# A retention layer and a snake-activated feed-forward layer on one core: a new order of the program up to block 1

## The chip, the core and the metric

The kernel runs on one core of one Trainium2 chip. The core has a matrix engine (PE, with its weight loads shown as PEld), a vector engine (DVE), a scalar engine (ACT), a general engine (POOL) and a sequencer that mostly issues DMAs (SP). Each engine works through its own list of instructions in order and waits on semaphores where it needs another's result. ACT, POOL and SP also issue DMAs from their lists. PE writes into PSUM, which the kernel uses as eight banks; POOL does not read them here. The metric is the time of one execution in microseconds (us), as the device counts it.

## What is computed

Shapes: q, k, v are 8 batches x 8 heads x 576 positions x 64. The output has 4608 rows (8 x 576) of 512. Cut to what matters:

```python
scores = scale * np.matmul(q, k.transpose(0, 1, 3, 2))
Dmat = np.where(rel >= 0, gamma[:, None, None] ** rel[None, :, :], 0.0)
attn_out = np.matmul(scores * Dmat, v)
x = attn_out.transpose(0, 2, 1, 3).reshape(B * S, H * D)    # 4608 x 512
h = x @ w_in                                                # 512 x 2048
g = h + np.sin(alpha * h) ** 2 / (alpha + 1e-09)
out = g @ w_out                                             # 2048 x 512
```

gamma is one number per head. Inputs and output are float32.

## The kernel before

Attention is done in chunks of 128 positions with a running state. For a batch b, the first 512 positions are handled as two halves p = 0, 1 of 256 positions, each two chunks; the last 64 positions of all batches form a ninth block at the end. The decay gamma^(i-j) is split into a factor on k and a factor on q, which a *cast* from float32 to float16 multiplies in.

For each batch and half the steps are: *load* k, q, v from HBM (512 KB each, on SP's list, into six rotating raw buffers, so that a load waits until the buffer six loads back has been cast); *cast* them (on V, that is DVE, on A_, that is ACT, or on G_, that is POOL; `ys=(0,)` or `(1,)` takes one half of the heads); *turn* k and q (PE transposes into a bank, 8 matmuls or 4 for one half) and *take* them back into SBUF (`kT`, `qT`); *outer* (64 x 64 products of k and v, the new sum of each chunk); *take_sum* or *evict* (the sum into `kvs`); *more* or *next_sum* (add the decayed former sum: two POOL instructions, or four DVE instructions); *to_state* (the sum times a factor, float16); *scores* (PE, for heads' half y, 16 matmuls); *masked* (DVE, the triangular mask, 128 x 1024 elements); *values* (PE, two passes) and *add_states* (PE, the state times q); *keep* (the result into `xT`, the input of the next layer). From batch 2 on the transposes of k and q are DMA transposes (*crossed*).

The feed-forward layer works on blocks n of 512 rows. *project(n, u)* makes unit u of 16 (128 of the 2048 hidden columns): four matmuls of 512 columns, into one PSUM bank; a third argument gives the bank (`op`, `h0`, `h1`, `h2`, `m0`, `m1`), a fourth one half of the rows. Then *sine* (ACT), *square* (ACT, DVE or POOL), *product* (DVE) write `gT`. *gemm2(n, u)* is the second layer for blocks 0 and 1: u = 4 c + part adds the hidden units 4 part to 4 part + 3 to output rows c, four matmuls of 512 columns; *finish* copies and stores a bank. Blocks 2 to 8 use a scheme with seven half-sized products in place of eight (`Quarters`), whose sums of weights *weigh* forms, on POOL mostly.

The weights are loaded by POOL: *load_w_in(g)* brings the columns of units 4 g to 4 g + 3, *load_w_out(g)* the rows of hidden units 4 g to 4 g + 3 (so gemm2 with part g), each 1 MB of float32 read and 512 KB of float16 written.

Nothing schedules the program: `tc.manual_schedule()` keeps the instructions of each engine in the order in which the Python calls stand, from line 740 on. The list up to line 1242 is written out by hand, block by block with batches ahead of it; a loop makes blocks 3 to 7. *keep_busy* issues matmuls on zeros, to fill PE. *told(last, eng)* puts an empty instruction on `eng` that waits for the instruction `last`; what follows on that engine waits with it.

Lines that matter here: load 121, cast 181 (k, q) and 104/102 (v, on DVE or POOL / on ACT), turn 215, outer 298, copies 102 and 104, next_sum 327, to_state 332, more 339 and 340, scores 358, masked 370, values 400, add_states 422, project 535, sine 543, square 552 (ACT) and 554, product 559, gemm2 581, weigh 602, load_w_in 92, load_w_out 95, keep_busy 696.

In the list before, batch 0's second q half is cast by POOL in one piece, w_in(0) and w_in(2) are issued after it, then `more(1)`; the first state of batch 0 is made on DVE; batch 1's second half of q is cast and turned while batch 0 is still being masked; the units of blocks 0 and 1 come in mixed orders (block 0: 2, 1, 0, 8, 3, 11, 6, 7, 5, 4, 12, 14, 9, 10, 15, 13).

## Time and profile before

| | us |
|---|---|
| median of 3 runs | 299.51 |
| lowest and highest | 299.17, 302.67 |
| the profiled execution | 301.28 |
| its span, first to last instruction | 299.6 |
| PE busy | 284.6 (95%) |
| DVE busy | 223.6 (75%) |
| ACT busy | 207.3 (69%) |
| POOL busy | 200.5 (67%) |

The mean granted clock of PE over the span is 0.983 of full speed.

How to read what follows. A *row of the timeline* gives start, duration, engine, source line, operation, the tiles (written <- read), shapes, how many instructions were merged, and in brackets how long the engine had been idle and what ended that. "SPq" is an instruction of SP's list. The *chain of waits* is followed back from the last instruction: each piece is the work that the next one waited for. A *list of waits* names who waited for whom: us in total, how often, the longest. A *table of stages* gives, for each stretch, the busy time of each engine, the granted clock, and the share and rate of the DMA engines. A *group* ("x14 | 10.1, 742 | 1.7") gives the count, the busy time in all, the mean ns of one and the idle time before. "DMA to landing" is the time from issue until the last byte was there.

### The profile page before, as it was taken

To read this page: it belongs to the slowest core of one execution; us is meant where nothing else is said; L and a number is where in the kernel's file an instruction comes from. 1 tells how busy PE (TensorE), PEld (TensorE's weight loads), DVE (VectorE), ACT (ScalarE), POOL (GpSimd) and SP (SyncE) were. 2 spreads that over 40 slices of the span, in tenths; PEclk is the share of its full clock that TensorE was granted. 3 is DMA by queue.
4 is the path that set the end of the run, shared out by engine and by line. 5 is a ranking of instruction groups with operands and counts; after the bars stand their busy time and mean duration, and the time that the engine had idled before them with its cause. 6 is when DMAs were issued, how large, how long until landed. Compare 5 with 4: busy or idle time off the path is not lost.

```text
span 299.6 us, 8720 instructions
## 1 busy us (share of the span) xinstructions
PE 284.6 (95%) x3597; PEld 185.3 (62%) x3597; DVE 223.6 (75%) x313; ACT 207.3 (69%) x330; POOL 200.5 (67%) x188
## 2 busy tenths in 40 slices
PE   7649999999999999989999999999999999999993
PEld 6536555554544576666666666766666666665782
DVE  1596899879867897998679867876778476656871
ACT  1434983886756799776878787878777878887600
POOL 5691675899999998898788889769923900370000
PEclk9787999999999999999999999999999999999999
DMA  7999999599888298878697977687866201310225
GB/s 220 341 216 216 279 233 287 151 287 287 229 172 263 63 153 185 225 194 191 152 267 184 190 189 204 57 183 161 151 137 145 53 3 39 71 37 16 62 49 120
DMA packets 119159, 49.89 MB, mean 167 GB/s; under 512 B 69824, under 2 KB 118096, under 8 KB 119120
## 3 DMA queue, kind: packets, MB, share of 16 engines
q1 hardware_dynamic: 114528, 45.04, 63.8%
q0 software_dynamic: 4224, 4.19, 8.3%
q8 instruction: 28, 0.46, 0.6%
q10 hardware_dynamic: 368, 0.11, 0.2%
q14 instruction: 11, 0.09, 0.1%
HBM read 36.74 MB, written 9.44 MB: 154 GB/s over the span
## 4 chain that ended last, share of the span: by engine, by line
PE 81%; DVE 6%; ACT 3%; POOL 3%; issue 2%; DMA 2%; SPq 1%; DVEq 0%; ACTq 0%
PE hps L535 37%; PE hps L652 27%; PE ops L581 9%; PE o L400 3%; ACT s_t L543 2%; PE sc L358 2%; DMA q<-in_q_dram 2%; DVE ret L370 2%; DVE gT L559 2%; DVE s L332 1%; PE kv L298 1%; SPq L121 1%; PE o L422 1%; POOL k L181 1%; POOL q L181 1%
## 5 line engine op out<-in xcount | busy, mean ns | idle before, releaser
L559 DVE SCALAR_TENSOR_TENSOR gT<-ss_t,inva,hps 128x512 f16<-128x512 f16 x144 | 105.5, 743 | 37.4 <-ACT ss_t L552 35.9
L543 ACT ACTIVATE s_t<-hps,alpha_t 128x512 f16<-128x512 f32 x144 | 96.5, 682 | 38.5 <-PE hps L535 37.8
L535 PE MATMUL hps<-xT,w_in 128*128 128x512 f16 (+1 forms) x564 | 121.4, 361 | 1.0 <-DVE gT L559 0.7
L535 PEld LDWEIGHTS <-w_in 128*128 128x128 f16 x628 | 60.5, 98 | 53.3 <-issue 1.8
L552 ACT ACTIVATE ss_t<-s_t 128x512 f16<-128x512 f16 x118 | 73.8, 630 | 3.2
L652 PEld LDWEIGHTS <-gT 128*128 128x128 f16 x656 | 63.9, 98 | 14.4
L624 POOL TENSOR_TENSOR gT<-gT,d 128x1024 f16<-128x1024 f16 x12 | 25.2, 2121 | 31.2 <-PE hps L652 30.2
L652 PE MATMUL hps<-T,gT 128*128 128x256 f16 x336 | 39.8, 273 | 0.0
L652 PE MATMUL hps<-w_out,gT 128*128 128x256 f16 x320 | 38.2, 273 | 0.0
L370 DVE TENSOR_TENSOR ret<-sc,mask 128x1024 f16<-128x1024 f32 (+1 forms) x32 | 34.8, 1115 | 3.0 <-PE sc L358 3.0
L672 DVE TENSOR_TENSOR osb<-osb,hps 128x512 f32<-128x512 f32 x35 | 24.0, 685 | 14.8 <-PE hps L652 14.1
L581 PE MATMUL ops<-w_out,gT 128*128 128x512 f16 x128 | 30.5, 379 | 0.2 <-ACT kvs L102 0.2
L181 POOL TENSOR_TENSOR q<-q,cn 128x1024 f16<-128x1024 f32 (+1 forms) x16 | 27.0, 1696 | 4.3 <-DMA q<-in_q_dram 4.3
L630 POOL TENSOR_TENSOR gT<-gT 128x1024 f16<-128x1024 f16 x12 | 26.1, 2195 | 0.0
L181 POOL TENSOR_TENSOR k<-k,cn 128x1024 f16<-128x1024 f32 (+1 forms) x13 | 21.9, 1684 | 2.3 <-DMA k<-in_k_dram 2.3
L581 PEld LDWEIGHTS <-gT 128*128 128x128 f16 x128 | 12.0, 98 | 13.9 <-issue 0.2
L340 POOL TENSOR_TENSOR kvs<-s,kvs 128x256 f32<-128x256 f32 x22 | 17.1, 777 | 2.5 <-ACT kvs L102 0.8
L102 ACT CAST xT<-o 128x1024 f16<-128x1024 f32 (+1 forms) x14 | 13.2, 956 | 6.5 <-PE o L422 6.5
L102 ACT COPY osb<-hps 128x512 f32<-128x512 f32 (+2 forms) x15 | 8.2, 548 | 13.6 <-PE hps L652 13.4
L332 POOL TENSOR_TENSOR s<-kvs,cn 128x256 f16<-128x256 f32 x21 | 13.4, 643 | 4.7 <-ACT kvs L102 4.0
L554 DVE TENSOR_TENSOR ss_t<-s_t 128x512 f16<-128x512 f16 x22 | 13.9, 631 | 3.3 <-ACT s_t L543 3.2
L535 PE MATMUL hps<-xS,w_in 128*128 128x512 f16 x64 | 15.0, 379 | 0.0
(78 smaller groups left out, 274.3 us busy)
## 6 DMA issues: line engine op xcount, KB each, us to landing
out_dram<-osb SPq DMA_DIRECT2D x70, 128.0 KB, 2.5
q<-in_q_dram SPq DMA_DIRECT2D x16, 512.0 KB, 5.7
k<-in_k_dram SPq DMA_DIRECT2D x10, 512.0 KB, 7.3
v<-in_v_dram SPq DMA_DIRECT2D x10, 512.0 KB, 6.0
k<-in_k_dram SPq DMA_DIRECT2D x24, 128.0 KB, 3.5
v<-in_v_dram SPq DMA_DIRECT2D x24, 128.0 KB, 3.5
w_in<-in_moe_w_in_dram POOLq DMA_DIRECT2D x4, 512.0 KB, 11.0
w_out<-in_moe_w_out_dram POOLq DMA_DIRECT2D x4, 512.0 KB, 10.2
```

The source lines that it names most:

```text
L102: eng.copy(d_, s_)
L181: eng.tensor_tensor(dst[:, a0:a1].rearrange("p a r t d -> p t (a r) d"), t_.rearrange("p (t a) x -> p t a x", t=2)[:, :, a0:a1].rearrange( ...
L370: nc.vector.tensor_tensor(ret.rearrange("p t (z x) -> p (t z) x", z=2)[:, :, 0:n], sc.rearrange("p t (z x) -> p (t z) x", z=2)[:, :, 0:n], ...
L535: matmul(hps_of[n, fc][0][:, cols], w_in16[:, a, fc * P : (fc + 1) * P], xs[n][:, a, cols], start=(a == 0 and part != 1), stop=(a == KT - ...
L543: nc.scalar.activation(s_t, hps, mybir.ActivationFunctionType.Sin, bias=0.0, scale=alpha_t[:, fc : fc + 1],)
L552: nc.scalar.activation(ss_t, s_t, mybir.ActivationFunctionType.Square)
L559: nc.vector.scalar_tensor_tensor(gT[n][:, :, fc, :], ss_t.rearrange("p (t n) -> p t n", t=2), inva[:, fc : fc + 1], hps.rearrange("p (t n) ...
L581: matmul(ops[n, c, cols.start][:, cols], gT[n][:, c // 2, fk, c % 2 * P : c % 2 * P + P], w_out16[:, fk, cols], start=(fk == 0), stop=(fk ...
L624: eng.tensor_tensor(self.part(0, 0, i), self.part(1, 1, i), self.d3[:, 4 * i : 4 * i + 4], SUB)
L630: eng.tensor_tensor(out_, self.part(1, 0, i), self.part(0, 0, i), SUB)
L652: matmul(self.ps[name][:, 256 * m + cols.start : 256 * m + cols.stop], left(j)[:, P * m : P * m + P], right(j)[:, cols], start=(tag is not ...
L672: nc.vector.tensor_tensor(out_, a, self.ps[ps], ADD)
```

## The change

The list from the first load to the end of block 1 is written anew; the rest changes only in unit numbers and in two gemm2 units that now stand earlier. `cast` returns its instruction, so that an engine can be made to wait for it, and batch 1's halves get the q buffers in natural order. In words:

- Batch 0 is cast, turned and taken by halves of the heads: k and q of the first half on DVE, v on DVE and ACT; the second q on POOL in two pieces, the second k on DVE in two. All six loads of batch 0 are issued first and the six of batch 1 directly behind them.
- An empty instruction makes POOL wait for the cast of the first q; then POOL issues w_in(0) and w_in(1), ahead of the second q. w_in(2) and (3) follow among batch 0's states, w_out(0) in block 0's unit 2, w_out(1) in unit 5, w_out(2) and (3) behind a cast of batch 1's first v.
- The states and all sums of batch 0 and batch 1 are made by POOL (`to_state`, `more`); the copies of batch 0's second sums stand ahead of keeping its first values.
- Batch 1 is turned and attended after block 0's projections, among fourteen gemm2 units of block 0 (nine before).
- Blocks 0 and 1 take their units in the order 0 to 15; in block 1, three gemm2 units of block 1 and two of block 0 stand where eight stood.

```diff
-    order_of_q = [(0, 0), (0, 1), (1, 1), (1, 0), (2, 0), (2, 1), (3, 1), (3, 0), (4, 1), (4, 0)]
+    order_of_q = [(0, 0), (0, 1), (1, 0), (1, 1), (2, 0), (2, 1), (3, 1), (3, 0), (4, 1), (4, 0)]
...
-            eng.tensor_tensor(
+            return eng.tensor_tensor(
...
         load(0, "k", 0)
         load(0, "q", 0)
-        cast(0, "q", 0, V, (1,))
+        load(0, "v", 0)
+        load(0, "q", 1)
+        load(0, "k", 1)
+        load(0, "v", 1)
+        cast(0, "k", 0, V, (0,))
         cast(0, "k", 0, V, (1,))
-        cast(0, "k", 0, G_, (0,))
...
         keep_busy(16, "h0", 256)
-        keep_busy(44, "op", 64)
+        keep_busy(14, "op", 64)
+        turn(0, "k", 0, "op", (0,))
+        take(0, "k", 0, A_, (0,))
+        keep_busy(3, "h0", 128)
+        turn(0, "k", 0, "op", (1,))
+        take(0, "k", 0, A_, (1,))
+        cast(0, "q", 0, V, (0,))
+        told(cast(0, "q", 0, V, (1,)), G_)
+        load_w_in(0)
+        load_w_in(1)
+        turn(0, "q", 0, "h2", (0,))
+        take(0, "q", 0, A_, (0,))
+        keep_busy(4, "h0", 128)
+        turn(0, "q", 0, "h2", (1,))
+        cast(0, "v", 0, V, (0,))
+        cast(0, "v", 0, A_, (1,))
+        take(0, "q", 0, V, (1,))
         at[0].outer((0,), "h0", "h1")
...
+        at[0].scores(0, 0, "m0")
+        at[0].scores(0, 1, "m1")
+        turn_alpha()
+        at[0].take_sum(0, A_)
+        take_alpha()
+        at[0].take_sum(1, A_)
+        at[0].masked(0, 0)
+        cast(0, "q", 1, G_, (0,))
+        cast(0, "q", 1, G_, (1,))
+        keep_busy(5, "h2", 256)
+        turn(0, "q", 1, "op", (0,))
+        take(0, "q", 1, A_, (0,))
+        at[0].to_state(0, G_)
+        cast(0, "k", 1, V, (0,))
+        cast(0, "k", 1, V, (1,))
+        turn(0, "k", 1, "h2", (0,))
+        take(0, "k", 1, A_, (0,))
+        turn(0, "q", 1, "op", (1,))
+        take(0, "q", 1, A_, (1,))
+        at[0].masked(0, 1)
+        turn(0, "k", 1, "h2", (1,))
+        take(0, "k", 1, V, (1,))
+        keep_busy(4, "h0", 256)
+        load(1, "k", 0)
+        load(1, "q", 0)
+        load(1, "v", 0)
+        load(1, "k", 1)
+        load(1, "q", 1)
+        load(1, "v", 1)
+        at[0].more(1)
+        cast(0, "v", 1, A_, (1,))
+        cast(0, "v", 1, G_, (0,))
+        at[0].scores(1, 1, "m0")
+        at[0].to_state(1, G_)
         load_w_in(2)
...
+        at[0].outer((1,), "h2", "op")
+        at[0].scores(1, 0, "m1")
+        at[0].masked(1, 1)
         at[0].masked(1, 0)
...
+        at[0].values(0, False, "h0", "h1")
         at[0].values(0, True)
         at[0].add_states(0)
+        at[0].take_sum(2, A_)
+        at[0].take_sum(3, A_)
+        at[0].keep(0, A_, A_)
+        at[0].more(2)
+        at[0].to_state(2, G_)
+        load_w_in(3)
+        at[0].values(1, False, "m0")
         at[0].values(1, True)
         at[0].add_states(1)
+        at[0].keep(1, A_, V)
+        project(0, 0, "op", 0)
+        project(0, 1, "h2", 0)
         invert_alpha()
+        at[0].more(3)
+        project(0, 0, "op", 1)
...
+        project(0, 4, "m1")
+        product(0, 2)
+        sine(0, 4)
+        cast(1, "k", 0, G_, (0,))
+        square(0, 4, G_)
+        project(0, 5, "m0")
+        sine(0, 5)
+        square(0, 5, A_)
         load_w_out(1)
...
+        project(0, 12, "h2")
+        sine(0, 12)
+        cast(1, "q", 0, G_, (0,))
+        square(0, 12, G_)
...
+        gemm2(0, 4, "op")
+        gemm2(0, 12, "h2")
+        turn(1, "q", 0, "m1")
         product(0, 15)
...
+        gemm2(0, 0, "h0")
+        at[0].to_state(3, G_)
+        at[1].scores(0, 0, "m0")
+        gemm2(0, 5, "op")
+        at[1].scores(0, 1, "m1")
+        at[1].masked(0, 0)
         at[1].masked(0, 1)
...
+        gemm2(0, 13, "h2")
+        cast(1, "v", 0, G_, (0,))
+        cast(1, "v", 0, A_, (1,))
+        load_w_out(2)
+        load_w_out(3)
+        gemm2(0, 1, "h0")
...
+        at[1].outer((0,), "m0")
+        at[1].evict((0,), A_)
+        cast(1, "k", 1, G_)
+        at[1].to_state(0, G_)
+        at[1].values(0, False, "m1")
+        at[1].values(0, True)
+        turn(1, "k", 1, "h1")
+        take(1, "k", 1, A_)
+        cast(1, "q", 1, V)
...
+        turn(1, "q", 1, "m0")
+        take(1, "q", 1, V)
         at[1].more(1)
         at[1].to_state(1, G_)
+        weigh(1, 0, G_)
+        cast(1, "v", 1, A_)
+        gemm2(0, 8, "h1")
+        at[1].scores(1, 1, "m0")
+        at[1].scores(1, 0, "m1")
+        at[1].masked(1, 1)
+        at[1].masked(1, 0)
+        gemm2(0, 9, "h1")
         gemm2(0, 6, "op")
+        at[1].outer((1,), "m0")
+        at[1].evict((1,), A_)
+        at[1].more(2)
+        at[1].to_state(2, G_)
+        gemm2(0, 14, "h2")
         at[1].values(1, False, "m1")
         at[1].values(1, True)
+        gemm2(0, 2, "h0")
         at[1].add_states(1)
         at[1].keep(1, A_)
+        gemm2(0, 10, "h1")
+        gemm2(0, 15, "h2")
+        finish(0, 3, V)
+        weigh(1, 1, G_)
+        gemm2(0, 7, "op")
...
+        project(1, 0, "m0", 0)
+        project(1, 0, "m0", 1)
...
+        project(1, 1, "h2")
+        square(1, 0, V)
+        sine(1, 1)
+        gemm2(0, 3, "h0")
...
+        gemm2(0, 11, "h1")
+        finish(0, 2)
...
-        gemm2(0, 8, "h1")
-        sine(1, 1)
+        gemm2(1, 0, "h1")
+        sine(1, 9)
...
-        gemm2(0, 9, "h1")
-        sine(1, 2)
+        gemm2(1, 1, "h1")
+        sine(1, 12)
...
-        gemm2(0, 10, "h1")
-        gemm2(0, 11, "h1")
-        finish(0, 2)
+        gemm2(1, 2, "h1")
...
         at[3].outer((0, 1), "m1")
         product(2, 3)
-        gemm2(1, 1, "h1")
-        gemm2(1, 2, "h1")
         at[3].evict((0, 1), A_)
```

More of the change, by code (lines that the diff above doesn't have):

```diff
@@ L781 @@
-        keep_busy(10, "h2", 256)
-        take(0, "q", 1, A_)
-        load(1, "q", 1)
-        at[0].take_sum(1, V)
-        at[0].more(1)
-        cast(0, "v", 1, V)
-        at[0].to_state(1, V)
-        load_w_in(1)
-        at[0].to_state(0, V)
-        at[0].outer((1,), "h2", "h1")
-        cast(1, "q", 1, G_)
-        at[0].masked(0, 1)
-        at[0].scores(1, 0, "m0")
-        turn(1, "q", 1, "op")
-        at[0].masked(0, 0)
-        at[0].masked(1, 0)
-        at[0].scores(1, 1, "m1")
@@ L901 @@
-        at[1].outer((0,), "h0", "h2")
-        at[1].masked(0, 1)
-        sine(0, 13)
-        at[1].scores(0, 0, "m1")
-        gemm2(0, 12, "h0")
-        gemm2(0, 13, "h0")
-        at[1].take_sum(0, A_)
-        at[1].take_sum(1, A_)
-        square(0, 13, A_)
-        at[1].masked(0, 0)
-        product(0, 13)
-        load(1, "v", 1)
-        turn(1, "k", 1, "h2")
-        take(1, "k", 1, V, (1,))
-        take(1, "k", 1, V, (0,))
-        gemm2(0, 14, "h0")
-        at[1].scores(1, 1, "m0")
@@ L918 @@
[L918 to L924 removed]
+        take(1, "q", 0, A_, (0,))
+        take(1, "q", 0, V, (1,))
+        gemm2(0, 0, "h0")
[4 more added lines that the diff above has]
+        at[1].masked(0, 0)
+        at[1].masked(0, 1)
```

309 lines of the change are left out of this document (111 added, 198 removed).

## The prediction

> **What bounds the kernel now.** I read first how long TensorE (PE) waited, then the stages, then the chain of the first 30 us, then the single rows. Waits of PE, in the first 28.3 us and from there to 113 us:
>
> ```profile
> PE sc L358 <- DVE ret L370: 3.8, 1, 3.8
> ...
> PE ops L581 <- ACT kvs L102: 0.2, 1, 0.2
> PE o L400 <- issue: 0.2, 1, 0.2
> ```
>
> Busy time by stage (columns: stretch, length, PE, weight loads, DVE, ACT, POOL, granted clock, DMA share, GB/s):
>
> ```profile
> 9.80:13.20 3.40, 3.21 (x59) 2.77 (x48) 2.04 (x4) 1.50 (x2) 3.13 (x3) 0.50 1.14 344
> 13.20:16.40 3.20, 3.10 (x83) 2.39 (x82) 1.90 (x4) 2.00 (x3) 3.08 (x5) 1.00 1.19 286
> 16.40:20.00 3.60, 0.00 (x0) 0.00 (x0) 3.60 (x3) 0.37 (x1) 3.52 (x4) 1.00 1.19 215
> 20.00:25.40 5.40, 5.03 (x128) 3.95 (x128) 4.76 (x5) 1.01 (x1) 3.53 (x4) 0.50 1.20 217
> 28.30:53.70 25.40, 25.06 (x345) 14.16 (x344) 23.33 (x44) 18.61 (x32) 15.00 (x17) 1.00 1.16 261
> 53.70:77.00 23.30, 23.30 (x245) 12.19 (x243) 20.52 (x27) 17.71 (x31) 22.83 (x22) 1.00 0.93 240
> 77.00:105.00 28.00, 27.73 (x471) 14.34 (x471) 21.39 (x27) 18.59 (x31) 27.61 (x29) 1.00 0.70 179
> ```
>
> From 28.3 to 113 us PE waits 0.4 us by the list: nothing that keeps its matmuls can gain there. All that can be gained lies ahead of 28.3 us, where PE stands still for 3.6 us (16.4 to 20.0) and then runs at half the clock. The chain of waits there:
>
> ```profile
> 4.00 6.01 DMA q<-in_q_dram
> 10.07 1.90 POOL q L181
> 11.97 1.47 POOL w_in L92 x2
> ...
> 15.41 3.50 DVE s L332 x2
> 18.92 3.41 DVE ret L370 x3
> ```
>
> Not a load but POOL's queue and DVE set the pace: the cast of q's second half, two weight DMAs issued ahead of a state sum, two states, four masks. The states' 3.50 us is odd:
>
> ```profile
> 15.41 3.50 DVE L332 TENSOR_TENSOR s<-kvs,cn 128x256 f16<-128x256 f32 x2 [1.30 <-POOL kvs L340]
> 16.15 1.91 POOL L181 TENSOR_TENSOR q<-q,cn 128x1024 f16<-128x1024 f32 x1
> 18.01 0.61 POOL L339 TENSOR_TENSOR s<-kvs,cn 128x256 f32<-128x256 f32 x1
> 18.84 4.72 DVE L370 TENSOR_TENSOR ret<-sc,mask 128x1024 f16<-128x1024 f32 x4
> L332 DVE TENSOR_TENSOR s<-kvs,cn 128x256 f16<-128x256 f32 x1 | 0.4, 417 | 0.0
> ```
>
> The same instruction takes 417 ns in a later stage; here the pair ends only after both POOL instructions, and the masks follow.
>
> **The change part by part.** I take it as one chain from batch 0's loads to T0, the start of block 0's first projection; from there I let PE run as densely as before from 28.3, and then look for what breaks that.
>
> *Batch 0.* The first six loads keep their order. The rows for the start:
>
> ```profile
> 5.57 1.04 POOL L181 TENSOR_TENSOR k<-k,cn 128x512 f16<-128x512 f32 x1 [1.47 <-DMA k<-in_k_dram]
> 7.03 0.69 DVE L181 TENSOR_TENSOR q<-q,cn 128x512 f16<-128x512 f32 x1 [5.80 <-DMA q<-in_q_dram]
> 8.51 1.04 ACT L102 CAST v<-v 128x1024 f16<-128x1024 f32 x1 [4.79 <-DMA v<-in_v_dram]
> 11.91 1.68 POOL L92 DMA_DIRECT2D w_in<-in_moe_w_in_dram  x2
> L121 SPq DMA_DIRECT2D k<-in_k_dram x1: 1460/1460/1460, 5.5 to 5.5; - x1
> DMA to landing us min/median/max: 6.0/6.0/6.0
> ```
>
> k, q and v are there at 5.6, 7.0 and 8.5, the second k at 5.5 + 6.0 = 11.5. DVE casts k's halves by 6.9 and q's by 8.3 (0.69 each). With turns, copies and v's halves on DVE and ACT about 9.5, the outer products run at 9.6 and both scores end by 11.1; before, the same scores were masked from 18.84. The first mask (4.72/4 = 1.2) runs 10.7 to 11.9. Then DVE casts the second k's halves while POOL casts the second q's halves (1.04 each, 10.1 to 12.1) and goes on to the states. If DVE gets its turn between two POOL instructions, the casts end at 13.8; mask 15.0, copy 15.4, scores 15.9, two masks 18.3, values 19.4. POOL's last state needed (to_state(2)) is about as late, 19.5. So T0 is 19.7.
>
> The row of 3.50 us says DVE may be passed over more than once, to about 14.8, and T0 to 20.7. The Trainium skill, "SBUF — State Buffer", section "SBUF: two separate sides", calls the port pair of the two engines an exclusive lock held for a whole instruction, which by itself gives the 19.7; the row, where DVE also sat out the second POOL instruction, measures worse than that. I take 19.7, since POOL here has gaps (it waits for sums); both ends stay in the range.
>
> *The weights.* The marker makes POOL wait for the second q cast (8.3); behind it stand w_in(0), w_in(1), q's casts, all states. Issued at 8.3 in place of 11.9, w_in(0) comes 3.6 us sooner:
>
> ```profile
> L92 POOL DMA_DIRECT2D w_in<-in_moe_w_in_dram x4: 746/804/942, 11.9 to 19.4; - x4
> DMA to landing us min/median/max: 7.8/11.0/11.8
> L121 SPq DMA_DIRECT2D v<-in_v_dram x1: 1350/1350/1350, 11.5 to 11.5; - x1
> DMA to landing us min/median/max: 14.1/14.1/14.1
> ```
>
> The first of the four needed the least, 7.8; the last, issued at 19.4, came 11 to 12 later: 19.7 to about 30.8, 3.7 apart. So w_in(0) now lands at 16.1, ahead of T0, and the next five weights, issued in time behind it, at about 20, 23.5, 27, 31 and 35, where units 4, 8 and 12 and the first gemm2 of either half want them at T0 + 3.5, 7, 10.5, 14.5 and 18: ahead each time. The price is paid by SP's queue, on which batch 1's six loads now stand directly behind batch 0's: rates fall from 344 to 215 GB/s when weights flow, and the v load issued at 11.5 needs 14.1 us where the k load at 5.5 needed 6.0. Batch 0's last v (due at 13.0) can lose up to some 2 us; its cast is needed by 15, so I cost it at 0, with 1.5 as the other end. Batch 1's first k, q and v are wanted at about T0 + 4, T0 + 10.6 and T0 + 15.5, and I put them at 22, 29.5 and 35: just in time. w_out(2) and (3), issued only after batch 1's first v is cast (about 36), would land near 45 and 49 at some 9 us and 4 us more (estimates from w_in's landing and the throttled rate), and the multiplications that need them come at 46 and 52: cover of 1 us, no more.
>
> *Block 0 and batch 1.* Sixteen projections in order, then fourteen gemm2 units among batch 1's attention, in place of nine. A unit of four matmuls costs 0.86:
>
> ```profile
> 59.12 0.86 PE hps L535 x4
> L559 DVE SCALAR_TENSOR_TENSOR gT<-ss_t,inva,hps 128x512 f16<-128x512 f16 x14 | 10.1, 742 | 1.7 <-ACT ss_t L552 1.5
> L554 POOL TENSOR_TENSOR ss_t<-s_t 128x512 f16<-128x512 f16 x4 | 4.1, 1036 | 10.6 <-ACT s_t L543 10.6
> ```
>
> DVE needs 16 x 0.742 plus five squares and a few copies, about 15.4 against PE's 13.8 plus turns; the lag of 1 to 2 us is taken up by six banks and by the gemm2 units that follow, so 0. No matmul of use is added or dropped. keep_busy costs nothing where PE would wait anyway; the units moved ahead of block 1 leave it (three gemm2 fewer, 20.7 of PE) with DVE at 20.5: DVE cannot hide less than that. Cost 0 to 2.6; I take 0.4.
>
> *POOL.* Net of what leaves it (half a cast of k, batch 1's q: 2.9), it gains two squares, two half casts of v, three sums and four states, about 9.3; so +6.4. Its waits before were longest at the squares (10.6 in the row above), so there is room in block 0. Before, this was its entry into batch 2:
>
> ```profile
> 53.39 4.09 POOL L104 CAST v<-v 128x1024 f16<-128x1024 f32 x2 [3.51 <-DMA v<-in_v_dram]
> 57.45 4.49 POOL L602 TENSOR_TENSOR T<-w_out 128x512 f16<-128x512 f16 x4
> 61.90 1.90 POOL L181 TENSOR_TENSOR q<-q,cn 128x1024 f16<-128x1024 f32 x1
> ```
>
> After, half of the T's (weigh(1, 0), 2.2) stands in a gap ahead, and from the copy of batch 1's last sums (25 units of 0.86, some 6 us of batch 1's small matmuls and the copy after T0: 48.1) come two sums and two states (3.9), the other half of the T's and the casts of v, 3.1 to 4.1: the q cast starts at 57.3 to 58.3 in place of 61.90. From there POOL is full: 22.83 of 23.30 and 27.61 of 28.00.
>
> *The sum.* Before, from 28.3 to the end of the span (299.6) is 271.3, with one unit of block 0 (0.86) and one of batch 1's four turns already done, which at full clock costs what the next one did:
>
> ```profile
> 31.77 0.61 PE L215 MATMUL tr<-ident,q 128*128 128x128 f16 x8
> ```
>
> After: 19.7 + 271.3 + 0.9 + 0.6 = 292.5, a gain of 7.1. Off that, 0.4 for DVE in block 1 and 0.3 for the clock (below): 6.4. The profiled execution took 301.28 with 299.6 as its span, 1.8 above the median of the runs, 299.51. Against the median, 299.51 - 6.4 = 293.1.
>
> **The rivals.** *POOL holds part of it back.* PE gains 7.1 by the sum, but POOL only 3.6 to 4.6 (61.9 less 58.3 or 57.3); if nothing in its full stretch to 105 us has slack, that less the clock's 0.3 stays: 295.2 to 296.2, and 297.2 with T0 at 20.7. Against it: in 28.3 to 113 us no wait of PE names POOL, and
>
> ```profile
> 73.43 1.18 POOL L332 TENSOR_TENSOR s<-kvs,cn 128x256 f16<-128x256 f32 x2
> 78.18 0.51 PE L422 MATMUL o<-qT,s 64*64 64x128 f16 x24
> ```
>
> batch 2's last state is ready 3.6 us ahead of the matmuls that read it (78.18 less 74.61).
>
> *POOL becomes the bound: slower.* The same engine, but its added 6.4 us finds no idle time, because in block 0 it waits in order behind casts of late loads. Then the cast of batch 2's second q starts at 61.9 + 6.4, and with 3.6 of slack the end moves by +2.8: 302.3. It decides once that cast starts after 65.5. Where DVE keeps interrupting POOL as it was itself held, the tail reaches past 305.5. For it: 98% busy; against it: ten us of idle time from 28.3 to 53.7 alone (15.00 of 25.40 busy).
>
> *The clock.* Batch 0 is now chopped into quarter steps with idle time between. The rows: the 3.6 us of standing still from 16.40 were followed by half clock (0.50 for 5.4 us), and the 3.40 us from 9.80, most of it turns, by full clock.
>
> ```profile
> 9.80:13.20 3.40, 2.90 (x24) 0.42 (x1) 1.50 (x2) 0.50 1.14 344
> ```
>
> (That is the turns' own tile: 2.90 of 3.40.) By these rows turns hold the clock up and the gaps after the change, at most 1.4, are short: 0.3. If they do not, PE starts block 0 at half clock for some 6.8 us, losing 3.4: 296.5. The Trainium skill, "TensorE: Matmul & The Clock Gate", "Part 4: PE-mode transpose", says that transposes do not count as busy for the clock; by that rule this case would come about, but the trace disagrees (1.00 after 9.80:13.20).
>
> **How the numbers follow.** My forecast has 0.58: 293.1, its own range 291 to 295.5 (from T0 half a us sooner and nothing taken off, 291.9, with the runs' own scatter below that, to T0 at 20.7 and half of DVE's 2.6). The faster bound, 2%, lies at 293.5; 0.45 of the 0.58 lies under it, since the late ends have to meet to pass it, 0.13 above. POOL holding back 0.16, the clock 0.10: both within 2%. POOL as the bound has 0.16, of which 0.12 beyond 305.5, where a POOL that cannot recover over 50 us ends, and 0.04 within. Faster by over 2% (about what a measurement of this kernel can tell from no change) 0.45, within 0.13 + 0.16 + 0.10 + 0.04 = 0.43, slower 0.12. The range for eight in ten runs from 291 to 298: it holds the first three cases and leaves out the slower one.
>
> **What would show it.** Right: the first projection on PE near 19.7 to 20.7; w_in(0) landed at 16; the four masks spread over 10.7 to 18.3; clock 1.00 from then on; PE's waits from T0 to block 2 under 1.5 us; POOL's first full q cast of batch 2 near 57. Wrong: a wait of PE on a DMA'd weight near gemm2 units 6 or 15, a POOL wait on k or q of batch 1, half clock in block 0, a projection's wait on DVE in block 1, or POOL late at that cast. A first projection after 23 would refute the chain for batch 0 as a whole.

## The result and the profile after

The change made the kernel slower. Three runs of the changed kernel took 313.15 to 315.29 us, 314.19 in the median, against 299.51 before: a ratio of 1.046, with an interval of 1.034 to 1.058. The prediction had 293.1 with a range up to 298. The span of the profiled execution after is 312.4; before it was 299.6.

The longest of PE's waits from 18 us to the end (total, times, longest, in us), of the changed kernel:

```profile
PE hps L535 <- DVE gT L559: 5.3, 3, 3.2
PE o L422 <- POOL s L332: 3.6, 2, 3.5
PE hps L535 <- issue: 1.6, 1, 1.6
PE sc L358 <- DMA qT<-q: 0.8, 1, 0.8
PE hps L652 <- DVE osb L672: 0.7, 1, 0.7
```

Before, the stretch from 28.3 to 113 us held 0.4 us of waits. Now there are long single ones: 3.2, 3.5 and, later, 1.6 us. The table of stages, after:

```profile
13.20:16.40 3.20, 2.30 (x101) 1.77 (x104) 2.68 (x4) 1.88 (x5) 3.12 (x5) 1.00 1.18 212
16.40:20.00 3.60, 2.51 (x82) 1.97 (x75) 1.63 (x3) 1.66 (x3) 3.40 (x6) 1.00 1.17 258
28.30:53.70 25.40, 21.81 (x292) 10.44 (x294) 17.51 (x21) 12.07 (x18) 16.87 (x21) 0.93 1.10 247
53.70:77.00 23.30, 22.16 (x232) 11.11 (x223) 18.72 (x25) 17.00 (x28) 12.35 (x12) 1.00 0.79 172
77.00:105.00 28.00, 23.97 (x326) 11.46 (x327) 17.05 (x22) 13.80 (x22) 27.29 (x30) 0.88 0.96 236
```

Read the column of PE and the granted clock together. The start is as wanted: the standstill of 16.4 to 20.0 is gone and the clock is full from 13.2 on. In 28.3 to 53.7 PE is busy 21.81 of 25.40 (25.06 before) at a clock of 0.93, in 77 to 105 23.97 of 28.00 (27.73 before) at 0.88, and between them POOL, which I had called full, works 12.35 of 23.30.

**The start.** The weights (group of w_in's four DMAs), the first projection on PE, the masks on DVE:

```profile
L92 POOL DMA_DIRECT2D w_in<-in_moe_w_in_dram x4: 746/803/942, 8.0 to 18.6; - x4
DMA to landing us min/median/max: 8.4/10.1/11.2
18.94 1.26 PE L535 MATMUL hps<-xT,w_in 128*128 128x256 f16 x10
10.06 1.23 DVE L370 TENSOR_TENSOR ret<-sc,mask 128x1024 f16<-128x1024 f32 x1 [0.77 <-PE sc L358]
15.36 2.36 DVE L370 TENSOR_TENSOR ret<-sc,mask 128x1024 f16<-128x1024 f32 x2 [0.52 <-PE sc L358]
```

w_in(0) is there at 8.0 + 8.4 = 16.4, the masks span 10.1 to 17.7, and the first projection runs at 18.94.

**First loss, block 0.** The timeline of POOL, DVE and PE around unit 7, and the clock of the stretch behind it:

```profile
27.48 1.05 POOL L554 TENSOR_TENSOR ss_t<-s_t 128x512 f16<-128x512 f16 x1
27.49 3.31 DVE L554 TENSOR_TENSOR ss_t<-s_t 128x512 f16<-128x512 f16 x1
28.48 1.04 POOL L181 TENSOR_TENSOR k<-k,cn 128x512 f16<-128x512 f32 x1
29.48 1.03 POOL L554 TENSOR_TENSOR ss_t<-s_t 128x512 f16<-128x512 f16 x1
32.30 1.02 PE L535 MATMUL hps<-xT,w_in 128*128 128x512 f16 x3 [3.16 <-DVE gT L559]
33.00:36.20 3.20, 3.20 (x9) 1.16 (x8) 2.22 (x4) 1.33 (x2) 0.77 (x1) 0.50 1.17 259
```

DVE's square of unit 7, which takes 0.43 us where POOL leaves it alone, begins 0.01 us after a square on POOL, and ends only when POOL's three instructions in a row are over: 3.31 us. PE waits 3.16 us for the products behind it, and then runs 3.2 us at half clock.

This is not what every square on DVE meets beside a busy POOL. The square of unit 3 in the same trace begins 0.52 us into a square on POOL, with a cast directly behind that one:

```profile
24.01 0.80 DVE L554 TENSOR_TENSOR ss_t<-s_t 128x512 f16<-128x512 f16 x1 [0.40 <-ACT s_t L543]
24.49 1.21 POOL L181 TENSOR_TENSOR k<-k,cn 128x512 f16<-128x512 f32 x1
```

It sits out the one POOL instruction and gets in ahead of the cast, which takes 1.21 in place of 1.04 us.

**Second loss, batch 2.** SP's own list of waits and its queue, then POOL, PE and the clock; below them one line of the kernel before, for the same load:

```profile
SPq L574 <- DVE osb L104: 9.4, 1, 9.4
57.84 2.47 SPq L574 DMA_DIRECT2D out_dram<-osb  x4
62.78 1.40 SPq L205 DMA_TRANSPOSE kT<-k  x1
64.50 1.41 SPq L205 DMA_TRANSPOSE qT<-q  x1
66.00 1.24 SPq L121 DMA_DIRECT2D q<-in_q_dram  x2
72.35 3.87 POOL L181 TENSOR_TENSOR q<-q,cn 128x1024 f16<-128x1024 f32 x2 [10.79 <-DMA q<-in_q_dram]
85.55 1.00 PE L422 MATMUL o<-qT,s 64*64 64x128 f16 x16 [3.46 <-POOL s L332]
84.00:90.80 6.80, 5.11 (x27) 1.95 (x28) 2.43 (x4) 1.54 (x2) 6.80 (x8) 0.50 1.12 234
```

```profile
57.12 1.15 SPq L121 DMA_DIRECT2D q<-in_q_dram  x2
```

SP stands 9.4 us in front of the store of block 0's fourth output, which `finish(0, 3, V)` copies on DVE. The transposes of batch 2 and the load of its second q stand behind that store and behind DVE's casts, which follow the same copy on DVE's list. So the load goes out at 66.00 (57.12 before), POOL is idle for 10.79 us, the cast of that q starts at 72.35 (61.90 before), the states are late, PE waits 3.46 us and loses the full clock for another 6.8.

**Third, block 3.** Two neighbouring rows of PE's timeline, and the instruction queue's row in the view of the DMA queues for 144.9 to 145.5 us:

```profile
145.31 0.39 PE L535 MATMUL hps<-xT,w_in 128*128 128x512 f16 x1
147.33 0.81 PE L535 MATMUL hps<-xT,w_in 128*128 128x512 f16 x3 [1.62 <-issue]
q8 instruction: 1, 0.02, 9.7%
```

Both rows are one projection of four matmuls, cut in two by a wait that nothing in the profile ends ("issue"); one block of instructions is fetched just ahead of it. The kernel before runs the four together.

### The profile page after: what moved, and what is told of

It is laid out like the page before. It is cut to its first block, busy times and chain, and to the rows that moved or that the text cites. A ratio compares the mean times of both kernels' runs of the same rounds, so it can differ in the third digit from the quotient of the medians.

```text
span 312.4 us, 8669 instructions
## 1 busy us (share of the span) xinstructions
PE 288.7 (92%) x3563; PEld 181.6 (58%) x3563; DVE 221.1 (71%) x301; ACT 208.6 (67%) x335; POOL 204.5 (65%) x201
## 4 chain that ended last, share of the span: by engine, by line
PE 78%; DVE 8%; POOL 4%; DMA 3%; ACT 3%; issue 2%; SPq 1%; DVEq 0%; POOLq 0%; ACTq 0%
PE hps L535 34%; PE hps L652 26%; PE ops L581 9%; DVE gT L559 4%; PE sc L358 3%; PE o L400 2%; DVE ss_t L554 2%; DMA v<-in_v_dram 2%; PE kv L298 2%; ACT s_t L543 1%; DVE ret L370 1%; PE o L422 1%; DMA k<-in_k_dram 1%; POOL s L332 1%; PE tr L215 1%
## 5 line engine op out<-in xcount | busy, mean ns | idle before, releaser
L559 DVE SCALAR_TENSOR_TENSOR gT<-ss_t,inva,hps 128x512 f16<-128x512 f16 x144 | 105.1, 744 | 44.9 <-ACT ss_t L552 43.5
L535 PE MATMUL hps<-xT,w_in 128*128 128x512 f16 (+1 forms) x556 | 123.6, 367 | 7.3 <-DVE gT L559 5.3
L535 PEld LDWEIGHTS <-w_in 128*128 128x128 f16 x620 | 59.7, 99 | 63.3 <-issue 9.4
L672 DVE TENSOR_TENSOR osb<-osb,hps 128x512 f32<-128x512 f32 x35 | 24.0, 686 | 19.0 <-PE hps L652 18.3
L181 POOL TENSOR_TENSOR q<-q,cn 128x1024 f16<-128x1024 f32 (+1 forms) x17 | 26.2, 1554 | 10.9 <-DMA q<-in_q_dram 10.8
L581 PE MATMUL ops<-w_out,gT 128*128 128x512 f16 x128 | 32.9, 396 | 0.3 <-DVE gT L559 0.2
L332 POOL TENSOR_TENSOR s<-kvs,cn 128x256 f16<-128x256 f32 x24 | 16.6, 692 | 11.6 <-ACT kvs L102 10.8
L181 POOL TENSOR_TENSOR k<-k,cn 128x1024 f16<-128x1024 f32 (+1 forms) x13 | 20.8, 1600 | 0.4 <-DMA k<-in_k_dram 0.4
L340 POOL TENSOR_TENSOR kvs<-s,kvs 128x256 f32<-128x256 f32 x24 | 18.2, 759 | 2.7 <-ACT kvs L102 0.9
L102 ACT CAST xT<-o 128x1024 f16<-128x1024 f32 (+1 forms) x16 | 14.5, 910 | 8.1 <-PE o L422 8.0
L554 DVE TENSOR_TENSOR ss_t<-s_t 128x512 f16<-128x512 f16 x21 | 16.3, 778 | 3.0 <-ACT s_t L543 2.8
L339 POOL TENSOR_TENSOR s<-kvs,cn 128x256 f32<-128x256 f32 x24 | 15.6, 652 | 0.2
## 6 DMA issues: line engine op xcount, KB each, us to landing
w_in<-in_moe_w_in_dram POOLq DMA_DIRECT2D x4, 512.0 KB, 10.1
w_out<-in_moe_w_out_dram POOLq DMA_DIRECT2D x4, 512.0 KB, 10.1
```

The source lines that it names most:

```text
L102: eng.copy(d_, s_)
L181: return eng.tensor_tensor(dst[:, a0:a1].rearrange("p a r t d -> p t (a r) d"), t_.rearrange("p (t a) x -> p t a x", t=2)[:, :, a0:a1].rea ...
L535: matmul(hps_of[n, fc][0][:, cols], w_in16[:, a, fc * P : (fc + 1) * P], xs[n][:, a, cols], start=(a == 0 and part != 1), stop=(a == KT - ...
L559: nc.vector.scalar_tensor_tensor(gT[n][:, :, fc, :], ss_t.rearrange("p (t n) -> p t n", t=2), inva[:, fc : fc + 1], hps.rearrange("p (t n) ...
L581: matmul(ops[n, c, cols.start][:, cols], gT[n][:, c // 2, fk, c % 2 * P : c % 2 * P + P], w_out16[:, fk, cols], start=(fk == 0), stop=(fk ...
L672: nc.vector.tensor_tensor(out_, a, self.ps[ps], ADD)
```

## The experiments

My theory was that these places, and not the change's start, made the kernel slower. Each of the times below is a median, and the ratio is to runs of the kernel before on the same chip. The expectations write GpSimd for POOL and ScalarE for ACT.

| | edit | us | ratio, interval |
|---|---|---|---|
| 1 | square 7 on ACT | 309.68 | 1.033, 1.028 to 1.039 |
| 2 | POOL: square 8 ahead of k's cast | 313.55 | 1.045, 1.038 to 1.053 |
| 3 | POOL: square 8 on ACT | 318.07 | one run |
| 4 | batch 2's casts and loads ahead | 311.99 | 1.038, 1.029 to 1.046 |
| 5 | 1 and 4 | 304.67 | 1.017, 1.010 to 1.023 |
| 6 | 1, and q's load ahead on SP alone | 309.15 | 1.030, 1.023 to 1.037 |
| 7 | 5, and 34 more warm-up matmuls | 302.74 | 1.005, 1.001 to 1.008 |
| 8 | before, 34 fewer warm-up matmuls | 305.14 | 1.017, 1.007 to 1.026 |
| 9 | the new start on the list of before | 314.35 | 1.047, 1.039 to 1.055 |
| 10 | 7, work from POOL to ACT and DVE | 301.99 | 1.007, 1.003 to 1.010 |
| 11 | before, the same relief | 300.03 | 1.001, 0.997 to 1.004 |
| 12 | 7, work from POOL to ACT alone | 301.65 | 1.004, 1.000 to 1.008 |

### The square that takes 3.3 us

**1.** The square is taken from DVE.

```diff
-        square(0, 7, V)
+        square(0, 7, A_)
```

> Unit 7's square goes from DVE to ACT; nothing else changes. Theory (DVE passed over by POOL): in the changed kernel that square, 0.43 us elsewhere, took 3.31 because three POOL instructions stood back to back; PE then waited 3.16 us for a product and ran the next 3.4 us at half clock. Without it the wait of 3.16 goes, the clock stays at 1.00, block 1's first projection starts near 53 in place of 57.8, and the time falls by 4 to 5 us, from 314 to about 309.5. Rival (DVE is simply full in block 0): one instruction of 0.43 less is worth under 1 us, and another wait of PE on a product takes its place: 313 to 314.

Measured 309.68, 4.5 less. The wait of 3.16 and the half clock behind it are gone; the wait on POOL's state in batch 2 stays.

**2.** POOL's order alone.

```diff
-        cast(1, "k", 0, G_, (1,))
         square(0, 8, G_)
+        cast(1, "k", 0, G_, (1,))
```

> Only POOL's order changes: the cast of batch 1's first k, second piece, goes behind unit 8's square instead of ahead of it, so that POOL has a gap of about half a us between unit 6's and unit 8's square while it waits for the sine. The same work on every engine. Theory (DVE is passed over as long as POOL's instructions stand back to back): unit 7's square on DVE gets in at the gap and takes under 1.2 us, the wait of 3.16 goes, 309 to 310. Rival (held for a fixed single instruction, or DVE full): the square stays above 2 us or the wait comes back at the next one, 313 to 314.

Measured 313.55: a miss. DVE's square again, and POOL's three instructions:

```profile
27.50 3.32 DVE L554 TENSOR_TENSOR ss_t<-s_t 128x512 f16<-128x512 f16 x1
27.50 2.04 POOL L554 TENSOR_TENSOR ss_t<-s_t 128x512 f16<-128x512 f16 x2
29.49 1.04 POOL L181 TENSOR_TENSOR k<-k,cn 128x512 f16<-128x512 f32 x1
```

The gap that I had counted on between POOL's squares does not exist: sine 8 was done in time, the three stand in a row as before, and DVE's instruction ends behind the third as before.

**3.** So the third instruction is taken away from POOL, and DVE's square is left where it is.

```diff
-        square(0, 8, G_)
+        square(0, 8, A_)
```

> The changed kernel, with block 0's square 8 on ScalarE in place of GpSimd; the rest as it is. GpSimd then has square 6 and the half cast of k back to back, and after them waits for sine 10. Theory (DVE's square of unit 7 is passed over as long as GpSimd's instructions stand back to back, and gets in at the first one that GpSimd has to wait for): the square takes about 2.3 us in place of 3.31 and ends shortly after the cast of k does, near 29.8; PE's wait for gT at 32.3 falls from 3.16 to about 2.1. Rival (the square is held by its own operand or by the loads of that time, and GpSimd only happens to be busy): it stays at 3.2 to 3.4. Time: 312 to 314 against 314.2 of the changed kernel, too little to tell; the records decide.

```profile
27.70 2.33 DVE L554 TENSOR_TENSOR ss_t<-s_t 128x512 f16<-128x512 f16 x1
27.68 1.05 POOL L554 TENSOR_TENSOR ss_t<-s_t 128x512 f16<-128x512 f16 x1
28.69 1.04 POOL L181 TENSOR_TENSOR k<-k,cn 128x512 f16<-128x512 f32 x1
30.96 1.04 POOL L554 TENSOR_TENSOR ss_t<-s_t 128x512 f16<-128x512 f16 x1 [1.23 <-ACT s_t L543]
```

Two POOL instructions in a row in place of three, 2.33 us in place of 3.31, the end at 30.0 just behind the cast: as the theory had it. The time (318.07, one run) lies above the 312 to 314 that I had expected; the profile shows another wait of PE, 2.7 us on DVE's kT. That is the same loss at a second place: DVE's next square, begun at 38.77 beside POOL's two issues of w_out, took 3.46 us, until the cast of k behind them was over, and the copy to kT stood behind it.

### Batch 2's second q

**4.** The two casts of batch 2's k and q on DVE, their transposes and the loads behind them go ahead of `gemm2(0, 10, "h1")`, and so ahead of the copies and stores of block 0.

```diff
+        cast(2, "k", 1, V, (0,))
+        cast(2, "k", 1, V, (1,))
+        load(3, "k", 1)
+        cast(2, "k", 0, V)
+        crossed(2, 0, "k")
+        cast(2, "q", 0, V)
+        crossed(2, 0, "q")
+        load(2, "q", 1)
+        load(3, "q", 1)
         gemm2(0, 10, "h1")
...
```

> Batch 2's casts of second k, first k and first q on DVE, the two transposes and the loads of the second q of batches 2 and 3 go ahead of the last gemm2 units and of block 0's first stores; POOL's order is the same. Theory (the load of batch 2's second q comes late because it stands on SP behind transposes that wait for DVE casts, which stand behind a store's copy): that cast starts on POOL near 62 in place of 72.35, POOL's wait of 10.8 us goes, and with it PE's wait of 3.5 for a state and the half clock of 84 to 91 that follows: 8 to 11 us less, 303 to 306. Rival (POOL's added 6.4 us of work is what comes late): POOL's wait for the load shrinks but PE still waits for the state; under 3 us less, 311 or more.

Measured 311.99, half a miss: the state wait of 3.5 us is gone, but the first loss is still in, and PE has a new wait on DVE.

```profile
PE tr L215 <- DVE kT L104: 2.8, 1, 2.8
39.55 3.56 DVE L554 TENSOR_TENSOR ss_t<-s_t 128x512 f16<-128x512 f16 x1
40.89 1.92 POOL L181 TENSOR_TENSOR k<-k,cn 128x1024 f16<-128x1024 f32 x1
```

This wait ends at 43.5, in a part of the list that the edit leaves alone. It is the loss of experiment 3's second place: a square on DVE, begun 0.21 us after POOL's two issues of w_out (39.34), ends only behind the cast that follows them, and the copy to kT comes after it. In the changed kernel the same square, begun 0.13 us after the same issues, was not held:

```profile
39.55 0.42 DVE L554 TENSOR_TENSOR ss_t<-s_t 128x512 f16<-128x512 f16 x1
```

So between 0.42 and 3.56 lies, as far as the rows show, a tenth of a us in when the square began. The profile is of one execution; how often the square is held there isn't known.

**5.** The edits of experiments 1 and 4 together.

> The square of unit 7 on ACT and batch 2's casts early, together. If the two losses are separate and are all that went wrong, the gains add: 298 to 301, at or under the kernel before. If the gain of the early start is lost in some third place, the sum stays at 303 or more and the trace of this kernel shows where PE waits.

Measured 304.67: 9.5 less than the changed kernel, where the two edits alone gave 4.5 and 2.2. The q cast is 13 us earlier than in the changed kernel:

```profile
59.36 3.76 POOL L181 TENSOR_TENSOR q<-q,cn 128x1024 f16<-128x1024 f32 x2 [0.63 <-DMA q<-in_q_dram]
```

Together the edits give more than the two alone; experiment 4's own profile had the second held square in it, and this one has not. More than 303, so there was a third place.

**6.** Is it the place on SP's queue, or DVE's casts too? Edit 1, and the load moved on SP alone.

```diff
+        load(2, "q", 1)
         crossed(2, 0, "k")
...
-        load(2, "q", 1)
```

> The changed kernel with square 7 on ScalarE (309.68, 1.0334 of the kernel before), and the load of batch 2's second q moved on SP's queue ahead of the two transposes of batch 2's first halves; DVE's casts stay behind the copy of block 0's last output. Theory (GpSimd's late cast of that q is set by where its load stands on SP's queue): the load is issued near 58.5 in place of 61.86, the cast starts at 64.5 to 65.5 in place of 68.05, PE's waits on states fall from 4.3 to under 2, and the time to 306 to 308 (1.021 to 1.028). Rival (the transfers of that time are the limit, and the load lands near 69 whenever it is issued, or the transposes behind it come late instead): 309 to 311.

```profile
64.92 1.90 POOL L181 TENSOR_TENSOR q<-q,cn 128x1024 f16<-128x1024 f32 x1 [7.64 <-DMA q<-in_q_dram]
69.68 1.90 POOL L181 TENSOR_TENSOR q<-q,cn 128x1024 f16<-128x1024 f32 x1 [2.87 <-DMA q<-in_q_dram]
PE sc L358 <- DMA qT<-q: 2.2, 1, 2.2
```

The cast starts at 64.92, as expected, and PE's waits on states fall from 4.3 to 0.7; but the time is 309.15, no gain that shows. The transposes are late in turn (2.2), and the next q is late too. The whole list behind the store was late; one entry passed forward pushes the others back.

### Where PE's list of instructions is divided

In the changed kernel and in experiments 1 to 6 the wait called "issue" stood at the same place, between the 1752nd and the 1753rd matmul. The kernel before has 34 more matmuls ahead of that point.

**7.** Experiment 5 with 34 more warm-up matmuls in the same number of columns.

```diff
-        keep_busy(16, "h0", 256)
+        keep_busy(48, "h0", 86)
...
-        keep_busy(5, "h2", 256)
+        keep_busy(7, "h2", 183)
```

> The kernel with square 7 on ScalarE and batch 2's casts ahead (304.67), with 34 more warm-up multiplications at the start in the same number of columns (48 of 86 in place of 16 of 256, 7 of 183 in place of 5 of 256), so that PE's list is as long as that of the kernel before. In all five kernels so far with the changed list PE stands 1.5 to 2.0 us in block 3 between the 1752nd and the 1753rd matmul, inside one projection, waiting for nothing that the profile shows, half a us after a 16 KB transfer of the instruction queue has begun; the kernel before has no such wait. Theory (PE runs out of instructions there, and where it does depends on how many stand ahead): the wait of 1.64 goes, and the time falls by that, to 302.7 to 303.3. Rival (the wait belongs to that projection: its bank, its operands): it stays at the same projection, 304 to 305.5.

Measured 302.74, and the wait is gone: as expected.

**8.** The kernel before with 34 fewer.

```diff
-        keep_busy(44, "op", 64)
+        keep_busy(10, "op", 282)
```

> The kernel before, with 34 fewer warm-up multiplications in the same number of columns (10 of 282 in place of 44 of 64), so that PE's list is as long as the changed kernel's; nothing else. Theory (the wait in block 3 comes from where PE's list of instructions is divided): a wait of 1.5 to 2.0 us without a releaser appears between the 1752nd and the 1753rd matmul in block 3, and the time rises to 301.0 to 301.5. Rival (it belongs to the changed order): no such wait, 299.3 to 299.8.

```profile
135.37 0.38 PE L535 MATMUL hps<-xT,w_in 128*128 128x512 f16 x1 [0.71 <-DVE gT L559]
137.31 0.82 PE L535 MATMUL hps<-xT,w_in 128*128 128x512 f16 x3 [1.56 <-issue]
```

The wait appears in a kernel that never had it, again behind the 1752nd matmul. The time rose by more than the wait (305.14): another "issue" wait of 0.68 us and one of 0.71 on DVE account for part of it, and the rest is not settled. That other "issue" wait stands behind the 1368th matmul, 384 ahead of the first; in experiment 4 one of 0.43 stands behind the 1369th, and in experiment 3 one of 0.66 behind the 2136th, 384 further on. Such a regular distance also speaks for a division by count and against one projection.

### The start alone

**9.** The changed start up to the copies of batch 0's values, with batch 1's loads in the old order, and from there the list of before.

```diff
         at[0].keep(1, A_, V)
-        project(0, 0, "op", 0)
-        project(0, 1, "h2", 0)
...
+        project(0, 2, "m1", 0)
+        project(0, 2, "m1", 1)
+        sine(0, 2)
+        project(0, 1, "op")
...
```

> The changed start alone: batch 0 by halves, w_in issued early, batch 1's six loads behind batch 0's, up to the copies of batch 0's values; from the first projection on the kernel before, unit by unit, with batch 1's first q turned a little later and its loads in the order in which that list wants them. PE's list is made as long as that of the kernel before by more warm-up multiplications. Theory (the start's lead is real, and what was lost was lost by the new order behind it): the first projection near 19 to 20, no DVE square over 1.5 us in block 0, batch 2's second q cast before 60, and 294 to 297. Rival (what follows the start has no room whichever way it is ordered: the transfers come when they come and DVE, ScalarE and GpSimd are full): the lead is gone by block 3, 299 to 303.

Measured 314.35: the rival, and worse than its 299 to 303. PE's timeline:

```profile
25.18 2.77 PE L535 MATMUL hps<-xT,w_in 128*128 128x256 f16 x16 [2.02 <-DMA w_in<-in_moe_w_in_dram]
35.58 3.21 PE L535 MATMUL hps<-xT,w_in 128*128 128x512 f16 x8 [5.46 <-ACT qT L102]
```

The old list wants a later quarter of w_in and batch 1's q at once, and those come when they come: the first projection starts at 19.14, and the lead is gone in these waits. So the early start does not pay with the old order behind it. The changed order, mended in three details (7), comes to 302.74, so most of what the change lost, it lost in details of that order.

### What is left: POOL

From the cast of batch 2's second q on, POOL of experiment 7 hardly pauses (from 73 to 103.1 us it is busy for 28.07 of 30.10). Rows of that run around its last state of batch 3, on POOL, PE, ACT and DVE:

```profile
103.14 0.60 POOL L332 TENSOR_TENSOR s<-kvs,cn 128x256 f16<-128x256 f32 x1
103.80 0.31 PE L422 MATMUL o<-qT,s 64*64 64x128 f16 x8 [0.61 <-POOL s L332]
103.78 0.58 ACT L102 COPY kvs<-kv 128x512 f32<-128x512 f32 x1 [1.98 <-POOL s L332]
104.92 0.75 DVE L559 SCALAR_TENSOR_TENSOR gT<-ss_t,inva,hps 128x512 f16<-128x512 f16 x1 [2.44 <-ACT ss_t L552]
114.39 1.89 PE L535 MATMUL hps<-xT,w_in 128*128 128x512 f16 x8 [1.37 <-DVE gT L559]
```

One late state holds PE for 0.61 us, ACT's copy for 1.98, and through ACT's square DVE for 2.44. PE's wait of 1.37 at 114 may be its last effect.

**10.** Work is taken from POOL ahead of it.

```diff
-        cast(3, "v", 0, G_, (0,))
+        cast(3, "v", 0, A_, (0,))
...
-        cast(3, "v", 1, G_, (1,))
+        cast(3, "v", 1, A_, (1,))
...
-        weigh(3, 1, G_)
+        weigh(3, 1, V)
...
-        weigh(2, 1, G_)
+        weigh(2, 1, V)
```

> The kernel of the last experiment but two (square 7 on ScalarE, batch 2's casts ahead, 34 more warm-up multiplications: 302.74, 1.0049 of the kernel before), with work taken off GpSimd between 73 and 92 us: its two half casts of batch 3's v go to ScalarE, and weigh(3, 1) and weigh(2, 1), four sums of 128x512, go to DVE, some 6 us of GpSimd's records in all. Theory (what is left of the loss is GpSimd's: from the cast of batch 2's second q on it works without a gap, 42.5 us to the last state of batch 3, and that state, at 103.1 here and 101.9 before, holds PE, then the copy of batch 4's sums, ScalarE's square, DVE's product): that state is ready by 101, PE's waits of 0.61 for it and of 1.37 for gT at 114.4 go, and the time falls by 1.5 to 2.5 us, to 0.996 to 1.000 of the kernel before. Rival (DVE and ScalarE are just as full there, or GpSimd's next work then waits for batch 4's loads): no gain, 1.003 to 1.008.

Measured 301.99, a ratio of 1.007: no gain. The state starts at 97.3, and the two waits on it are gone, but

```profile
83.85 1.05 PE L581 MATMUL ops<-w_out,gT 128*128 128x512 f16 x3 [1.26 <-DVE gT L559]
```

stands where experiment 7 had nothing: DVE, with the sums on it, is late with a product.

**11.** The same edits on the kernel before.

> The kernel before with the same four edits and nothing else. Theory: in it no wait of PE from 28 to 134 us names GpSimd, whose last state of batch 3 is ready 1.3 us ahead of the matmuls that read it; so the relief frees GpSimd and moves the end by nothing, 0.997 to 1.003 of the kernel before. Rival (GpSimd sets the pace there too): it gains 1.5 us or more, below 0.995.

Measured 300.03, a ratio of 1.001: nothing, as expected. Before, POOL is just as full and never late.

**12.** Only the two casts of v, to ACT.

> The kernel of the seventh experiment (302.74, 1.0049 of the kernel before) with GpSimd's two half casts of batch 3's v on ScalarE, and nothing given to DVE: 1.4 us of GpSimd's records. Theory (the relief before this one failed because the sums given to DVE made products late): GpSimd's last state of batch 3 starts near 101.7 in place of 103.1, PE's wait of 0.61 for it goes, its waits on DVE before 90 stay at 1.3 as in the seventh, and the time falls by 0.5 to 1.5, to 1.000 to 1.003. Rival (ScalarE's copies wait there and make it late in turn): 1.005 or more.

The state starts at 100.23 and the waits at 103.8 and 114.4 are gone, but 301.65 is a ratio of 1.004 where experiment 7 had 1.005, and the intervals overlap: the gain isn't shown. No version of the changed kernel that I ran is faster than the kernel before.

## Why the prediction was wrong

**Right.** The chain of batch 0: first projection at 18.94 (forecast 19.7), w_in(0) at 16.4 (16.1), masks 10.1 to 17.7 (10.7 to 18.3). The clock behind the first turns: 1.00 from 13.2 to the first loss, so the rival of the clock did not come about there. The weights were in time: no wait of PE from 18 us on names w_in or w_out. In the start, where the forecast let DVE get its turn between two POOL instructions, it did: its two casts of the second k took 2.17 us from 11.2, each behind one POOL instruction.

**Wrong, first step: "the lag of 1 to 2 us is taken up by six banks and by the gemm2 units that follow, so 0".** I added up DVE's instructions at the durations that they have alone. The same prediction had read, in the start of before, that two of DVE's states took 3.50 us because DVE sat out two POOL instructions, and I had kept that reading to batch 0. The change gives POOL two more squares and half casts in block 0, back to back, and one of DVE's squares met them: 3.31 in place of 0.43 us, 3.16 of PE's time, and the clock behind it. Taking that square from DVE gave back 4.5 us (experiment 1), and its length followed the number of POOL's instructions in a row (3). How often it would happen could not be read from the row of 3.50: in the fourteen traces of this case, 107 squares on DVE began while POOL worked and had another instruction directly behind; 101 of them sat out one POOL instruction at most, and six sat out two or three. Why those six is not settled. Four of them, all of unit 7, began less than 0.02 us after a square on POOL; the other two beside issues of w_out. The Trainium skill, "SBUF — State Buffer", section "SBUF: two separate sides", names the kind of instruction that is held, two SBUF inputs on DVE against a POOL instruction that reads SBUF; the traces agree: DVE's product, which reads a PSUM bank, took 0.74 us beside the same POOL squares. That the loser waits for one instruction, as that section has it, agrees with the 101, but is not what the 3.31 shows.

**Wrong, second step: "the q cast starts at 57.3 to 58.3 in place of 61.90".** I worked that out from POOL's own list, as if its load were there. In the kernel before that load goes out at 57.12, and its cast follows within 5 us, so even then POOL could not have cast at 57.3. After the change, the load stood on SP behind a store that waited 9.4 us for a copy on DVE, and behind transposes whose casts stood behind the same copy. The step asked, of the loads, only about batch 1's and the weights, and left out that `finish(0, 3, V)` now stands ahead of batch 2's casts and transposes. Part of the delay is the first loss passed on: with it mended (1), the load goes out at 61.86, still 4.7 us later than before, and PE's wait for the state is still 3.4. The cast came at 72.35, beyond the 65.5 that I had named as the point from which POOL makes it slower; but not by the mechanism of that rival, since POOL was idle 10.79 us and not overfull. Moving the casts and loads ahead gave back 5.0 us on top of experiment 1 (5).

**Wrong, third step: "no matmul of use is added or dropped"**, taken to mean that PE's time is the same. The same paragraph of the prediction put the warm-up matmuls at nothing. 34 of them fewer shifted the places where PE's list is divided, one of them into block 3, behind a stretch of short matmuls. That cost 1.4 to 2.0 us in every kernel with that count and went when the count was restored (7), and came in the kernel before when the count was taken from it (8). That the count decides is shown; why this division costs time and others do not is not. The short matmuls ahead of it are one candidate, the DMA queues another: in the changed kernel one queue, with the transposes of k in it, took 85% of the DMA engines' time from 144.9 to 145.5, when the block was fetched.

**Mis-sized: the lead of 7.1 us.** With the first two losses mended (experiment 5), PE starts block 1 at 54.2 with fourteen gemm2 units done; before, at 53.7 with nine. Five units of 0.86 less the 0.5 are 3.8 us of lead, not 7.1. Waits in block 0 and batch 1 that were each under 0.35 us, and batch 1's small matmuls, which now stand singly between gemm2 units, are candidates; which of them it was, I did not test.

Added up against the forecast span of 293.2 (292.5, with 0.4 and 0.3 taken off the gain): block 0 3.16 and half of 3.2; batch 2 3.46, 0.8 and half of the 5.1 us that PE worked at half clock; the "issue" wait 1.6; the two other waits on gT and the one on osb, 2.8, less the 0.7 that stood there before; and 3.3 of the lead. That is 18.6 of the 19.2 us by which the span of 312.4 is off. It is an account by rows and not a proof: for the first two losses it has 4.8 and 6.8, where mending them gave back 4.5 and 5.0.

The three edits of experiment 7 bring the ratio from 1.046 to 1.005. That kernel starts block 1 at 54.2 with the lead of 3.8 us and yet ends some 1.5 us behind the kernel before; where these 5 us go, between block 1 and the end, is open.

**The rival "POOL holds part of it back"** is what remained behind these losses: in experiment 7 POOL's late state costs PE 0.61 us directly, and all its waits on states 1.3. That it sets the end is not shown, since moving its work away (10, 12) gave no gain beyond the interval.

## What to carry to other kernels

When work moves between engines, ask of each instruction that comes to stand beside it what it does to that neighbour's duration: a sum of durations measured alone says nothing of a square beside a full POOL, and a shift of a tenth of a us may decide whether it is held. When an instruction is moved on one engine, follow each in-order queue that waits for it, and for a cast ask first when its load is issued. And a wait that names nothing, at the same instruction in every variant, may lie in where the program is cut into blocks and not in its logic: change the number of instructions ahead of it and see whether it goes.

## What the runs showed of the hardware

- A square on DVE with both inputs in SBUF, 0.43 us alone, mostly sat out one POOL instruction and got in ahead of the next, even where the two stood directly behind each other (0.80 at 24.01, with POOL's next cast lengthened from 1.04 to 1.21). In six cases it sat out more: 3.31, 3.32 and 3.32 us behind three in a row (the changed kernel, experiments 2 and 4), 2.33 behind two (3), and 3.56 and 3.46 beside two issues of w_out and a cast (4 and 3). At unit 7, reordering POOL's instructions changed nothing; leaving it one fewer did.
- Behind the 1752nd matmul PE stood 1.4 to 2.0 us in all eight profiles whose list has 3563 matmuls, and not at all in the six whose list has 3597. The wait began 0.4 to 0.9 us after the instruction queue's transfer of 16 KB had started. The Trainium skill, "Runtime: NRT & Kernel Launch", section "Instruction fetch mechanics", says that the instructions come in blocks of 16 KiB, 256 instructions each, fetched while the one before is worked off, and mostly hidden; the traces agree on the size of the block, and show a place where it isn't hidden.
- After a standstill of PE the granted clock fell to 0.50 in most cases, not in all: for 3.2 us behind 3.16, for 6.8 behind 3.46 (the changed kernel), for 3.3 behind 3.4 (experiment 1, from 81.3) and for 3.2 behind 2.8 (experiment 4, from 43.2). Behind the 3.16 of experiment 2 it stayed at 1.00 (32.5 to 36.2). By the sum above, the half clock cost 1.6 us after the first and 2.6 after the second.
